# A written-out instruction order searched again, with GpSimd's memory-matrix product counted as making VectorE wait

## The chip, the cores and the metric

The kernel runs on one core of one Trainium2 chip. The core has five engines with queues of their own, each of which runs its instructions in order: TensorE (PE) multiplies matrices, VectorE (DVE), ScalarE (ACT) and GpSimd (POOL) do elementwise work, and SyncE (SP) issues the transfers (DMAs). The metric is the device time of one execution in microseconds, here 441.84 us as the median of three runs.

## What is computed

One transformer block over 2048 tokens of width 576. The attention half has 32 heads of width 18 and takes the tokens in four segments of 512. Every segment does causal softmax attention within itself, and reads a memory matrix that the earlier segments have filled:

```
for s in range(4):
    p = softmax(q_s k_s^T * scale + causal mask)
    a_dot = p v_s
    a_mem = phi(q_s) M / (phi(q_s) z + 1e-6)      # phi(t) = t + 1 if t > 0, else exp(t)
    out_s = g * a_mem + (1 - g) * a_dot           # g = sigmoid(beta), one number for each head
    M += phi(k_s)^T v_s ;  z += sum(phi(k_s))
h  = x + concat(out) wo
h2 = h + gelu(layernorm(h) w1 + b1) w2 + b2       # w1: 576 to 4608, w2: 4608 to 576
```

Data are bf16, sums and normalizations are in float32.

## The kernel before

**Stages.** The kernel is cut into 1904 operations. Each has a tag (stage and segment) and a name; the third number of a name counts its occurrences within the tag, from 0. Stage X normalizes and transposes x; P projects it to k, q and v; A is attention (`A00` to `A03` for the four token tiles of segment 0, `A1` to `A3` for the later segments); M sums the memory; B is the output projection, the residual and the second normalization; C is the first half of the MLP (`F1` its matmuls, `copy` the evictions, `gelu`); D is the second half (`F2`). The segments overlap: while segment 0 is in its MLP, segments 1 to 3 are in their projections and attention.

**Who sets the order.** No planner runs at the time of the launch that could choose. `TIMETABLE` gives every operation its engine and its place in one list of 1904 places: in `"A00mask": "g114 g147 g145 d104 ..."` the fourth mask (`A00mask.3`) is on VectorE (d) at place 104. The letters are p TensorE, a ScalarE, d VectorE, g GpSimd, s SyncE; w means that the operation is done in one instruction with its neighbour, u that ScalarE evicts with the gelu at once and no gelu follows. `schedule()` walks the list, gives out buffers (PSUM banks, tiles) in its order and emits the instructions; each engine's queue is the list cut down to its own operations. A place is therefore an order, not a time. The list was found beforehand by a search that used the same `schedule()` as its cost model.

**The model's rule on the shared port.** `Op` sets `rest`: how long an operation occupies the port to SBUF that VectorE and GpSimd share, that is its cost less a part at its start. `schedule()` lets an operation with a `rest` begin that part only when no operation with a `rest` on the other engine is in its own. An operation whose name stands in neither of the two lists has no `rest`, and neither waits nor makes wait.

**The memory-matrix product.** `mblk` (line 1085, stage M, three times) multiplies the summed memory by the gates into `MZ_blk`, four products of 18 partitions by 152 elements on GpSimd. `mem` (lines 1282 and 1285) is the matmul that reads it in the next segment's attention.

**Names that the steps below use.** `P..P` and `P..R` with k, q, v or o: the two halves of a projection of one token tile (lines 924, 954, 971). If both halves are neighbours in TensorE's order, they become one fused group, mostly eight full-row matmuls (line 954) and two of 64 rows (line 924); otherwise both are done in halves of the rows, 18 matmuls of 64 rows (line 924), and a small `pass` sits between them. `P..copy` evicts a projection; `fk` (line 1042), `ek` and `rk` make phi(k). `st0`, `exp`, `mask`, `val` are the scores, exponentials, causal masks and value products (lines 1151, 1102 and 1100, 1163 on VectorE and 1166 on GpSimd, 1182); in the later segments `st`, `exp`, `mask`, `val` (1311, 1336). `valT`, `rec`, `comb`, `swap` and `oT` bring the attention's output into the layout that the projection `Po`/`Ro` takes. `hadd` (1393) adds the residual; `stats`, `rstd` and `apply` are the normalization. `memset`, `ones`, `eps`, `gmz` prepare constants; `gates` is the sigmoid of beta.

Of the kernel before, what the change touches and what calls it, by code (L numbers as in the profile page):

```python
# [27 lines left out]
    "A00exp": "a 74 78 103 111",  # L28
    "A00mask": "g114 g147 g145 d104 g166 g192 d131 g190",
    "A00st0": "p 73 102",  # L30
    "A01comb": "g 200 211 250 234",
    "A01exp": "a151 a152 a155 a167 a179 w193 a175 a176",
    "A01mask": "g163 d156 g158 g162 d188 d198 g207 d194",
    "A01oT": "d 206 231 255 254 251",
    "A01rec": "d 186 202 223 217",
    "A01st0": "p 136 154 178 171",
    "A01swap": "g247 d242",
    "A01val": "p 172 208",
    "A01valT": "d 185 187 215 209",
    "A02comb": "g350 d399",  # L40
    "A02exp": "a197 a216 a260 w268 a218 a219 a235 w237 a288 w289 a308 a309 a338 a339",
    "A02mask": "g277 g278 g274 g281 g279 g305 g341 d340",
    "A02rec": "d 333 386",
    "A02st0": "p 196 252 210 229 275 296 320",
    "A02val": "p 304 325 352 354",
    "A02valT": "d 326 355",
    "A03comb": "g 487 513",
    "A03exp": "a361 a362 a390 w392 a369 a371 a400 a401 a413 a414 a423 w437 a463 w470",
    "A03mask": "d404 g375 g370 g372 g412 g416 g464 g478",
    "A03oT": "d 351 406 508 521 538",  # L50
    "A03rec": "d 430 481",
    "A03st0": "p 360 374 366 398 405 422 435",
    "A03swap": "d514 g523",
    "A03val": "p 417 418 477 479",
    "A03valT": "d 426 480",
    "A1comb": "d667 g694 g717 g782 g807 g816 g860 d883",
    "A1comb2": "g689 g703 g721 d783 g838 d824 d880 d888",
    "A1eg": "a 493 393 522 688 651 719 742 813",
    "A1exp": "a491 w501 a506 w516 a499 a500 a589 a594 a529 a530 a603 a610 a628 w631 a641 w650 a663 a679 a686 w693 a711 w723 a745 a751 "
        "a727 w734 a766 w770 a784 w789 a754 a757 a820 a826 a829 a839 a842 a849 a793 w799",  # L60
    "A1flip": "s 391 389 486 439 510 615 704 738",
    "A1mask": "g502 g536 g586 g584 g545 g605 d611 g604 g646 g671 g658 d672 g708 g700 g722 g714 d748 g752 g756 g773 d743 g781 g795 d790 "
        "g845 g830 g837 g840 g852 d850 g821 g809",
    "A1mem": "p 585 475 681 735 713 798 843 855",
    "A1memT": "d 593 476 691 736 718 808 844 856",
    "A1memfin": "g622 g647 g720 g767 d763 d823 d866 g882",
    "A1oT": "d 780 797 905 892 897",
    "A1pq": "d 550 428 642 710 662 771 803 831",
    "A1rec": "d 607 636 697 747 762 822 857 881",
    "A1rec2": "d 666 624 701 741 787 815 854 870",  # L70
    "A1rg": "g 454 410 596 547 660 765 778 788",
    "A1st": "p 483 505 498 582 528 602 625 640 657 685 707 744 726 764 777 749 814 828 836 792",
    "A1swap": "d 893 895",
    "A1val": "p 587 621 687 739 774 796 851 861",
    "A1valT": "d 599 623 698 740 776 811 853 869",
    "A2comb": "d1037 d983 d1143 g1096 g1175 g1190 g1246 d1230",
    "A2comb2": "d1039 d1067 d1146 g1097 d1188 g1193 d1259 d1236",
    "A2eg": "a 928 872 1053 976 1003 1085 1137 1160",
    "A2exp": "a899 a901 a858 w859 a886 a887 a874 a875 a906 a907 a993 w996 a1013 w1019 a985 a986 a1033 w1048 a1001 w1006 a1086 w1098 "
        "a1056 w1057 a1109 w1110 a1064 w1065 a1120 a1124 a1129 a1130 a1135 w1140 a1184 a1185 a1156 w1158 a1164 w1165",  # L80
    "A2flip": "s 825 847 891 961 1002 1040 989 1121",
    "A2mask": "d938 d915 d963 g903 d911 g958 g909 d923 g1042 d1032 g1041 g1007 g987 g1049 g1023 g1046 g1106 d1062 g1071 d1112 d1144 "
        "g1088 g1149 g1147 g1161 g1199 d1180 g1218 d1186 g1200 g1197 d1179",
    "A2mem": "p 998 946 1066 1044 1131 1145 1194 1202",
    "A2memT": "d 1011 960 1081 1047 1132 1148 1195 1212",
    "A2memfin": "g1038 d973 g1111 d1095 d1187 g1173 d1256 d1216",
    "A2oT": "d 1115 1178 1232 1263 1267",
    "A2pq": "d 951 910 1054 997 1075 1091 1170 1177",
    "A2rec": "d 1015 972 1090 1080 1154 1159 1231 1213",
    "A2rec2": "d 1036 982 1094 1073 1162 1152 1245 1229",  # L90
    "A2rg": "g 947 894 924 962 1074 1087 999 1176",
    "A2st": "p 898 848 885 873 904 988 1012 974 1020 1000 1084 1055 1105 1063 1116 1122 1134 1181 1155 1163",
    "A2swap": "g1238 d1265",
    "A2val": "p 970 959 1043 1050 1127 1150 1219 1201",
    "A2valT": "d 984 980 1072 1051 1128 1151 1226 1203",
    "A3comb": "g1426 d1376 d1481 d1503 d1556 g1528 g1642 d1611",
    "A3comb2": "g1427 d1445 g1499 d1504 g1572 d1563 g1643 g1617",
    "A3eg": "a 1211 1266 1337 1429 1474 1458 1543 1550",
    "A3exp": "a1220 w1224 a1250 w1254 a1262 a1269 a1334 a1336 a1279 a1280 a1389 a1390 a1372 a1384 a1396 a1397 a1412 a1415 a1362 a1366 "
        "a1443 w1444 a1423 w1424 a1463 w1467 a1492 a1495 a1452 w1454 a1507 a1510 a1518 a1524 a1532 w1539 a1567 a1569 a1547 a1548",  # L100
    "A3flip": "s 1141 1123 1282 1306 1208 1446 1387 1525",
    "A3mask": "g1268 d1341 d1356 d1313 d1351 g1350 d1342 g1298 d1418 g1410 g1393 g1406 d1409 g1416 g1398 g1403 d1491 d1468 d1461 d1493 "
        "g1479 d1496 g1482 g1455 d1590 g1554 g1553 g1540 g1565 g1570 d1579 d1587",
    "A3mem": "p 1340 1330 1425 1460 1526 1516 1586 1593",
    "A3memT": "d 1346 1331 1435 1473 1527 1523 1604 1600",
    "A3memfin": "g1365 g1364 g1477 d1502 g1571 g1542 g1619 d1602",
    "A3oT": "d 1451 1533 1646 1645 1644",
    "A3pq": "d 1253 1326 1405 1450 1498 1506 1578 1562",
    "A3rec": "d 1347 1354 1436 1489 1549 1541 1609 1601",
    "A3rec2": "d 1392 1375 1480 1478 1530 1515 1641 1610",  # L110
    "A3rg": "g 1227 1325 1377 1430 1209 1505 1559 1551",
    "A3st": "p 1217 1249 1261 1333 1278 1380 1371 1395 1408 1349 1437 1421 1459 1484 1447 1501 1517 1531 1566 1546",
    "A3swap": "d 1622 1621",
    "A3val": "p 1363 1352 1422 1431 1494 1497 1599 1595",
    "A3valT": "d 1374 1373 1441 1462 1500 1511 1640 1597",
    "B00Po": "p 256",
    "B00Ro": "p 258",
    "B00T": "p 306 348",
    "B00apply": "d 286",
    "B00copy": "a 315 349",  # L120
    "B00dma": "s 220 557",
    "B00hadd": "d264 w265",
    "B00pass": "d 257",
    "B00rstd": "g 285",
    "B00stats": "d 266",
    "B00tail": "d 287",
    "B01Po": "p 262",
    "B01Ro": "p 269",
    "B01T": "p 334 345",
    "B01apply": "d 322",  # L130
    "B01copy": "d 337 346",
    "B01dma": "s 248 436",
    "B01hadd": "d270 w271",
    "B01pass": "g 263",
    "B01rstd": "g 321",
    "B01stats": "d 298",
    "B01tail": "d 323",
    "B02Po": "p 554",
    "B02Ro": "p 560",
    "B02apply": "d 627",  # L140
    "B02dma": "s 497 896",
    "B02flip": "s 728 737",
    "B02hadd": "d568 w574",
    "B02pass": "g 559",
    "B02rstd": "g 626",
    "B02stats": "d 601",
    "B02tail": "d 680",
    "B03Po": "p 548",
    "B03Ro": "p 558",
    "B03apply": "d 620",  # L150
    "B03dma": "s 445 664",
    "B03flip": "s 684 702",
    "B03hadd": "d561 w562",
    "B03pass": "g 551",
    "B03rstd": "g 588",
    "B03stats": "d 567",
    "B03tail": "g 652",
    "B1Po": "p 912 925 929 940",
    "B1Ro": "p 914 931 935 942",
    "B1apply": "d 937 1025 1014 1083",  # L160
    "B1dma": "s 871 927 884 1028 953 1108 967 1010",
    "B1flip": "s 968 1021 1070 1092 1079 1076 1103 1104",
    "B1hadd": "d919 w920 d933 w943 d965 w966 d969 w971",
    "B1pass": "d913 g926 g930 d941",
    "B1rstd": "g 936 977 1004 1082",
    "B1stats": "d 921 952 991 1060",
    "B1tail": "g956 g1031 d1022 d1089",
    "B2Po": "p 1286 1290 1281 1303",
    "B2Ro": "p 1294 1300 1284 1305",
    "B2apply": "d 1309 1428 1464 1381",  # L170
# [169 lines left out]
    "omg": "g 174",  # L340
    "ones": "a 38 16",
    "tri": "g 5",
    "warm": "p 12 20 21",
    "wodma": "s 125 130",
    "x0b": "a 1",
    "x1": "s 2",
# [1391 lines left out]
```

## Time and profile before

| What | Value |
|---|---|
| runs of the kernel | 441.43, 441.84, 442.7 us (median 441.84) |
| the profiled execution, its own time | 441.8 us |
| its span, first to last instruction | 439.9 us |
| TensorE clock granted | 1.0 throughout |
| TensorE busy | 431.1 us, 98% of the span, 5069 matmuls |
| VectorE busy | 279.7 us, 64%, 578 instructions |
| ScalarE busy | 294.7 us, 67%, 314 instructions |
| GpSimd busy | 173.2 us, 39%, 331 instructions |
| transfers | 70.09 MB, mean 159 GB/s |

The profile's timeline has a row for each run of like instructions: start and duration in microseconds from the start of the span, engine, line of the kernel, operation, output from input with shapes, the count, and in brackets how long the engine stood idle before it and what ended that wait. Rows with a count over 1 cover all instructions of the run. The table by windows gives, for a stretch of the span, the busy time of PE, of its weight loads (PEld), of DVE, ACT and POOL, each with its number of instructions, then the granted clock, the share of the DMA engines and GB/s.

### The profile page before, as it was taken

What the parts mean: (1) busy time and instruction counts of PE and PEld (TensorE: products, weight loads), DVE (VectorE), ACT (ScalarE), POOL (GpSimd) and SP (SyncE); (2) the same over time, 40 slices, a digit from 0 to 9 for tenths busy, and PEclk for the clock granted to TensorE, in tenths of its full rate; (3) what the DMA queues carried; (4) which work ended last, traced back from release to release, by engine and by line L of the source; (5) the groups of instructions that cost most, each with busy time, mean ns of one, the idle gap of its engine ahead of it and who ended that gap; (6) DMA issues with size and microseconds to landing.
All of it is one profiled execution on the core that took longest, in us unless ns stands there. A gap on an engine that the chain in (4) does not pass through costs nothing.

```text
span 439.9 us, 12070 instructions
## 1 busy us (share of the span) xinstructions
PE 431.1 (98%) x5069; PEld 275.5 (63%) x5069; DVE 279.7 (64%) x578; ACT 294.7 (67%) x314; POOL 173.2 (39%) x331
## 2 busy tenths in 40 slices
PE   8988999999999999999999999999999999999997
PEld 5755678766677676654445766644457785446775
DVE  6999998897888885888797768876525021000111
ACT  6998888999977897677997877667842002656000
POOL 5686867655866252564331255352211110000000
PEclk9999999999999999999999999999999999999999
DMA  7899599899989965573746273616516553510102
GB/s 246 172 230 269 203 248 281 137 195 267 178 303 266 348 136 142 114 160 93 214 125 187 91 139 73 137 46 225 165 53 192 153 127 97 191 59 1 40 1 68
DMA packets 77126, 70.09 MB, mean 159 GB/s; under 512 B 58000, under 2 KB 64528, under 8 KB 77072
## 3 DMA queue, kind: packets, MB, share of 16 engines
q1 hardware_dynamic: 76928, 69.23, 60.8%
q8 instruction: 39, 0.64, 0.6%
q14 instruction: 15, 0.12, 0.1%
q10 hardware_dynamic: 144, 0.09, 0.1%
HBM read 42.30 MB, written 13.37 MB: 127 GB/s over the span
## 4 chain that ended last, share of the span: by engine, by line
PE 88%; DVE 7%; DMA 2%; issue 1%; ACT 1%; SPq 0%; DVEq 0%; ACTq 0%
PE bank L1563 31%; PE bank L1466 24%; PE bank L1509 7%; PE bank L924 7%; PE bank L954 5%; PE bank L1311 4%; PE bank L1336 3%; PE bank L971 1%; DMA w1g<-in_B_w_dram 1%; DVE ln L814 1%; PE bank L748 1%; DVE fk_pad L1042 1%; DMA ot<-in_B_b_dram 1%; PE bank L1285 1%; PE bank L1151 1%
## 5 line engine op out<-in xcount | busy, mean ns | idle before, releaser
L1563 PEld LDWEIGHTS <-hT 128*128 128x128 bf16 x1152 | 110.3, 98 | 34.1 <-issue 6.7
L1466 PE MATMUL bank<-xreg,w1g 64*128 64x512 bf16 x972 | 107.8, 376 | 0.0
L1102 ACT ACTIVATE pt<-bank 128x1024 bf16<-128x1024 f32 x88 | 85.2, 1022 | 24.2 <-PE bank L1311 14.9
L1466 PEld LDWEIGHTS <-w1g 64*128 64x128 bf16 x972 | 46.2, 94 | 56.7 <-issue 3.0
L1100 ACT ACTIVATE pt<-bank 128x2048 bf16<-128x2048 f32 x36 | 67.6, 1877 | 17.6 <-PE bank L1311 10.2
L1563 PE MATMUL bank<-w_lo,hT 128*128 128x288 bf16 x576 | 77.2, 286 | 0.0
L1563 PE MATMUL bank<-w,hT 128*128 128x288 bf16 x576 | 76.9, 286 | 0.1
L1576 DVE TENSOR_TENSOR ot<-bank,hc 128x288 bf16<-128x288 f32 x32 | 14.1, 449 | 82.0 <-PE bank L1563 73.4
L1325 POOL TENSOR_SCALAR_AFFINE_SELECT pt<-pt 128x512 bf16<-128x512 bf16 x63 | 43.5, 699 | 48.5 <-ACT pt L1102 27.1
L1472 ACT ACTIVATE hT<-bank,b_col 128x512 bf16<-128x512 f32 x36 | 22.3, 688 | 48.0 <-PE bank L1466 47.6
L1509 PE MATMUL bank<-xreg,w1g 64*128 64x256 bf16 x648 | 38.5, 269 | 0.8 <-DVE hT L1523 0.6
L1432 ACT ACTIVATE hT<-hT 128x4096 bf16<-128x4096 bf16 (+6 forms) x12 | 34.0, 2866 | 2.6 <-DVE hT L1488 2.5
L1509 PEld LDWEIGHTS <-w1g 64*128 64x128 bf16 x648 | 31.1, 94 | 7.0 <-issue 3.2
L1482 ACT ACTIVATE hT<-bank,b_col 128x512 bf16<-128x512 f32 x40 | 25.3, 693 | 10.6 <-PE bank L1466 10.2
L954 PE MATMUL bank<-hT,xreg 128*128 128x288 bf16 x228 | 31.4, 287 | 0.0
L924 PE MATMUL bank<-hT,xreg 64*128 64x288 bf16 x340 | 26.2, 284 | 0.5 <-DVE qk_pad L739 0.5
L954 PEld LDWEIGHTS <-xreg 128*128 128x128 bf16 x228 | 20.9, 98 | 7.5 <-issue 1.2
L1311 PE MATMUL bank<-qk 32*128 32x512 bf16 (+3 forms) x384 | 23.8, 301 | 0.1
L1291 DVE STREAM_TRANSPOSE t<-bank 128x512 f32<-128x512 f32 x24 | 16.9, 704 | 8.1 <-PE bank L1282 5.2
L924 PEld LDWEIGHTS <-xreg 64*128 64x128 bf16 x340 | 16.2, 94 | 9.2 <-issue 5.5
L1344 DVE STREAM_TRANSPOSE t<-bank 128x512 f32<-128x512 f32 x24 | 16.6, 696 | 6.4 <-PE bank L1336 6.3
L830 POOL TENSOR_TENSOR ln<-ln,mhalf 128x1 f32<-128x1 f32 x32 | 18.6, 580 | 2.7
(129 smaller groups left out, 574.0 us busy)
## 6 DMA issues: line engine op xcount, KB each, us to landing
w1g<-in_B_w_dram SPq DMA_DIRECT2D x41, 576.0 KB, 5.0
qkd<-qk_pad SPq DMA_DIRECT2D x12, 512.0 KB, 3.6
hd<-h SPq DMA_DIRECT2D x16, 288.0 KB, 3.0
hc<-hd SPq DMA_DIRECT2D x16, 288.0 KB, 3.4
w_lo<-in_B_w_dram SPq DMA_DIRECT2D x3, 864.0 KB, 7.2
w<-in_B_w_dram SPq DMA_DIRECT2D x3, 864.0 KB, 6.7
xb<-in_A_x_dram SPq DMA_DIRECT2D x16, 144.0 KB, 4.1
out_dram<-ot SPq DMA_DIRECT2D x15, 144.0 KB, 2.8
```

Source lines behind the costliest of these rows:

```text
L924: return nc.tensor.matmul(out=half(hf), lhsT=xTb.t[r, k, ts], rhs=wt[r, hf, k, :], start=start, stop=stop, skip_group_check=True)
L954: nc.tensor.matmul(out=half(hf), lhsT=xTb.t[:, k, ts], rhs=wt[:, hf, k, :], start=(k == 0 and b.form != "first"), stop=(k == n - 1 and b.f ...
L1100: nc.scalar.activation(out=pt.t[:], in_=banks_all[:, st[0].n:st[0].n + 4, :], func=ACT.Exp, scale=scale)
L1102: nc.scalar.activation(out=pt.t[:, 2 * j:2 * j + 2, :], in_=st[j].t[:], func=ACT.Exp, scale=scale)
L1311: nc.tensor.matmul(out=st[i // 2].t[:, i % 2, off:off + n_], lhsT=qk[rows, 1, kt * P:(kt + 1) * P], rhs=qk[rows, 0, kt * P:L], start=True, ...
L1325: nc.gpsimd.affine_select(out=blk, in_=blk, pattern=[[0, 4], [1, P]], compare_op=ALU.is_ge, fill=0.0, base=0, channel_multiplier=-1)
L1432: nc.scalar.activation(out=at, in_=at, func=ACT.Gelu_apprx_tanh)
L1466: nc.tensor.matmul(out=cc[w].t[:], lhsT=w1.t[rows, k, q, :], rhs=x2T[s].t[rows, k, :], start=(k == 0), stop=(k == ND - 1))
L1472: ready_f[f + w] = [add(pf - 12, {"act": 0.68}, lambda e, f=f, w=w, cc=cc: nc.scalar.activation(out=hT[:, :, f + w, :], in_=cc[w].t[:].rea ...
L1482: nc.scalar.activation(out=dst, in_=src, func=ACT.Identity if e == "act" else ACT.Gelu_apprx_tanh, bias=b)
L1509: nc.tensor.matmul(out=cc[w].t[:, q * 2 * P:(q + 1) * 2 * P], lhsT=w1.t[rows, k, q, :], rhs=x2T[s].t[rows, k, ts], start=(k == 0), stop=(k ...
L1563: nc.tensor.matmul(out=c.t[:, 0:c1 - c0], lhsT=hT[:, tl // 2, f, (tl % 2) * P:(tl % 2 + 1) * P], rhs=w2_c[ch][:, f - ch * WCH, c0:c1], sta ...
```

## The change

The operations, their instructions and their dependencies are the same. One name is added to the list of GpSimd operations that occupy the shared port, and the whole timetable is replaced by one that a search found under that rule, beginning from the former. Counted over the whole list, VectorE has six masks and five evictions more, GpSimd six masks fewer and four `comb2` more; ScalarE and the rest differ by a handful. Most of the change is order. All places are numbered anew, so nearly every row differs; the rows below are those that the text speaks of.

```diff
-        g = 0.15 if name in ("mask", "comb", "comb2", "memfin", "rg", "rk", "hc", "rstd", "eps", "memset", "swap") else 0.0
+        g = 0.15 if name in ("mblk", "mask", "comb", "comb2", "memfin", "rg", "rk", "hc", "rstd", "eps", "memset", "swap") else 0.0
...
-    "A00mask": "g114 g147 g145 d104 g166 g192 d131 g190",
+    "A00mask": "g 100 139 152 121 122 180 138 192",
-    "P01copy": "d123 d137 d93 a87 a98 a138",
+    "P01copy": "d120 d145 a99 a90 a106 a132",
-    "X00copy": "a25 d33 a31 a35",
+    "X00copy": "a30 d31 d36 a37",
-    "X00apart": "d19 a23 d28 a29",
+    "X00apart": "d12 a22 d26 a32",
-    "P00Pk": "p 37 41",
+    "P00Pk": "p 39 40",
-    "memset": "d8 g7 g36 d65 a26 a94 a58 a109 g427 g14 g328",
+    "memset": "d43 g9 g21 d2 a29 a35 a56 a34 g44 g14 g0",
-    "ones": "a 38 16",
+    "ones": "a 13 69",
-    "eps": "g 79 72 319 421 447 331 330 329",
+    "eps": "g 16 441 15 253 38 327 380 385",
-    "gates": "a95 d169",
+    "gates": "a124 d174",
-    "X1apply": "d 214 173",
+    "X1apply": "d 230 176",
-    "P1copy": "d232 a241 a344 d177 a189 a233 d313 a327 a297 a253 a293 d385",
+    "P1copy": "d234 a250 a344 d168 a204 a229 d314 a326 a304 a267 a295 d382",
-    "A02mask": "g277 g278 g274 g281 g279 g305 g341 d340",
+    "A02mask": "g259 g252 g316 g266 g291 g262 g338 d347",
-    "P1rk": "g 300 230 368 357",
+    "P1rk": "g 269 248 406 355",
-    "X2stats": "d 284 261 365 356",
+    "X2stats": "d 283 265 365 359",
-    "P1fk": "d 301 259 419 358",
+    "P1fk": "d 301 268 407 356",
-    "B00hadd": "d264 w265",
+    "B00hadd": "d270 w271",
-    "A02st0": "p 196 252 210 229 275 296 320",
+    "A02st0": "p 203 249 216 235 281 300 324",
-    "A02comb": "g350 d399",
+    "A02comb": "g 363 451",
-    "M0mblk": "g 448",
+    "M0mblk": "g 442",
-    "M1mblk": "g 484",
+    "M1mblk": "g 702",
-    "M2mblk": "g 1252",
+    "M2mblk": "g 965",
-    "X3apply": "d 457 532 539 443",
+    "X3apply": "d 454 530 561 504",
-    "P1Pq": "p 238 180 314 276",
+    "P1Pq": "p 238 188 320 284",
-    "P1Rq": "p 240 182 318 283",
+    "P1Rq": "p 242 195 322 286",
-    "P1Pk": "p 226 160 310 243",
+    "P1Pk": "p 231 162 306 241",
-    "P1Rk": "p 228 168 312 246",
+    "P1Rk": "p 233 165 313 247",
-    "A3val": "p 1363 1352 1422 1431 1494 1497 1599 1595",
+    "A3val": "p 1354 1360 1442 1445 1505 1507 1597 1598",
-    "C2F1": "p 1575 1573 1624 1616 1552 1544 1564 1536 1585 1582 1612 1606 1668 1630 1658 1628 1665 1635",
+    "C2F1": "p 1568 1588 1536 1548 1543 1550 1564 1571 1582 1600 1632 1658 1618 1610 1646 1626 1655 1669",
-    "A3oT": "d 1451 1533 1646 1645 1644",
+    "A3oT": "d 1589 1602 1622 1636 1638",
-    "A3swap": "d 1622 1621",
+    "A3swap": "a1625 d1631",
-    "B3Po": "p 1647 1666 1650 1648",
+    "B3Po": "p 1639 1657 1641 1670",
-    "B1Po": "p 912 925 929 940",
+    "B1Po": "p 908 911 927 943",
-    "B1Ro": "p 914 931 935 942",
+    "B1Ro": "p 912 922 934 945",
-    "B2Po": "p 1286 1290 1281 1303",
+    "B2Po": "p 1284 1295 1278 1292",
-    "B2Ro": "p 1294 1300 1284 1305",
+    "B2Ro": "p 1297 1300 1281 1301",
-    "B3Ro": "p 1652 1671 1656 1680",
+    "B3Ro": "p 1643 1665 1651 1672",
```

566 rows, old and new, of the table TIMETABLE are left out of this document.

## The prediction

> **What bounds the kernel now.** I read the page's engine shares first, then the busy times by windows, then TensorE's waits and the timelines around the longest.
>
> ```profile
> span 439.9 us, 12070 instructions
> ...
> PE 431.1 (98%) x5069; PEld 275.5 (63%) x5069; DVE 279.7 (64%) x578; ACT 294.7 (67%) x314; POOL 173.2 (39%) x331
> ```
>
> TensorE is the bound overall: 439.9 of span less 431.1 busy leaves 8.8 us. The windows say where they lie.
>
> ```profile
> 11.00:22.00 11.00, 10.92 (x164) 8.10 (x160) 10.08 (x23) 10.99 (x19) 6.94 (x22) 1.00 0.81 172
> 22.00:33.00 11.00, 9.30 (x213) 6.55 (x213) 10.76 (x24) 10.17 (x12) 9.12 (x18) 1.00 1.11 230
> 33.00:44.00 11.00, 9.60 (x130) 6.28 (x130) 10.70 (x24) 9.25 (x10) 7.18 (x15) 1.00 0.94 269
> 66.00:77.00 11.00, 10.41 (x214) 8.89 (x208) 9.87 (x20) 9.83 (x9) 7.77 (x20) 1.00 1.09 280
> 77.00:429.00 352.00, 351.63 (x3893) 218.96 (x3890) 208.31 (x419) 227.99 (x231) 119.54 (x202) 1.00 0.56 145
> ```
>
> TensorE idles 1.70 us between 22 and 33, 1.40 between 33 and 44, 0.59 between 66 and 77, and 0.37 in all of the 352 us that follow. Where it idles, VectorE is full (10.76 and 10.70 of 11) and ScalarE nearly so. A new order can therefore win in the first 77 us, by relieving VectorE; afterwards it can only lose, apart from what it takes from TensorE's own work. The end (last value of `F2`, its addition, its store) is in the same order in both lists, and is counted at nothing.
>
> **The rule itself.** The planner now lets `mblk` hold the port for its whole length. The trace shows what that hold does:
>
> ```profile
> 68.43 2.43 POOL L1085 TENSOR_TENSOR MZ_blk<-MZacc,gmz 18x152 bf16<-18x152 f32 x4
> 69.23 0.75 DVE L1275 SCALAR_TENSOR_TENSOR e<-e,r 128x512 bf16<-128x512 bf16 x1
> L1275 DVE SCALAR_TENSOR_TENSOR e<-e,r x24: 628/686/1165, 69.2 to 298.5; 128x512 bf16<-128x512 bf16 x24
> ```
>
> A two-input VectorE operation in the middle of `mblk` took 0.75 us against a median of 0.686: 0.06 lost, where the planner would charge up to 2. No TensorE wait follows it. So the rule corrects nothing that costs time; its effect is that the search found another list. I cost that list by its parts, from places and rows.
>
> **TensorE's own work.** Counted in the lists, 34 projections have both halves adjacent before and 31 after: `P1Pk.3`, `P1Pq.0`, `B1Po.0` and `B2Po.3` are split, `B3Po.3` is joined.
>
> ```profile
> 85.29 0.30 PE L924 MATMUL bank<-hT,xreg 64*128 64x288 bf16 x2
> 85.52 2.13 PE L954 MATMUL bank<-hT,xreg 128*128 128x288 bf16 x16
> 87.81 0.40 PE L1311 MATMUL bank<-qk 32*128 32x384 bf16 x8
> 88.14 2.38 PE L924 MATMUL bank<-hT,xreg 64*128 64x288 bf16 x36
> 90.36 0.78 PE L924 MATMUL bank<-wt_o,oT 64*128 64x288 bf16 x10
> ```
>
> Two fused projections run from 85.29 to 87.81, 1.26 us each; two split ones from 88.14 to 90.36, 1.11 each. Three times 0.15 is 0.45. A split one needs a `pass` in time, or another matmul between its halves; I take **-0.4** (0 to -0.6).
>
> **The stretch from 16 to 33 us.**
>
> ```profile
> 16.87 0.76 DVE L739 CAST v_aug<-bank 128x576 bf16<-128x576 f32 x1 [0.31 <-PE bank L924]
> 17.55 0.42 DVE L1163 TENSOR_TENSOR pt<-pt,tri 128x512 bf16<-128x512 bf16 x1
> 22.24 0.85 DVE L1163 TENSOR_TENSOR pt<-pt,tri 128x512 bf16<-128x512 bf16 x1
> 23.81 0.79 PE L924 MATMUL bank<-hT,xreg 64*128 64x288 bf16 x10 [0.49 <-DVE qk_pad L739]
> 26.86 0.47 DVE L1620 TENSOR_SCALAR g_bc<-g_bc 128x32 f32<-128x32 f32 x1
> 28.27 0.74 DVE L739 CAST qk_pad<-bank 128x576 bf16<-128x576 f32 x1
> 29.07 0.41 PE L1151 MATMUL bank<-qk 32*128 32x128 bf16 x16 [0.89 <-DVE qk_pad L739]
> 27.39 1.94 ACT L1102 ACTIVATE pt<-bank 128x1024 bf16<-128x1024 f32 x2 [0.46 <-PE bank L1151]
> 5.54 0.39 ACT L713 ACTIVATE fk_pad<-fk_pad 128x224 uint32<-128x224 uint32 x1
> 6.97 0.76 ACT L1608 ACTIVATE v_aug<-ident 128x128 bf16<-128x128 bf16 x1
> ```
>
> The first three rows are `P01copy.2`, `A00mask.3` and `A00mask.6`. The copy goes to ScalarE, the masks to GpSimd: 0.76 + 0.42 + 0.85 = 2.03 us leave VectorE ahead of its eviction that TensorE waits for at 23.81. The second wait, 0.89 at 29.07, is for `P1copy.3` at 28.27, which stands behind `gates` and `X1apply.1`, 26.86 to 28.27 or 1.41 us; in the new list it stands ahead of both. So both waits, 1.38 us, can go. What is late next is ScalarE. It gains that copy (some 0.7 by the row on VectorE) and `ones.1` (0.76, row at 6.97), which leaves a slot where ScalarE waited, and loses two clears of 0.39 (row at 5.54) to the start: 0.7 more in a stretch where it was busy 10.99 of 11 and whose only slack just before the second wait is 0.46, at 27.39. GpSimd has room for the two masks. I take **-0.7**, half of the 1.38 (0 to -1.38).
>
> **The start.** Here the moved work lands: on ScalarE two clears now stand ahead of `X00copy.3`, on GpSimd a large `memset` of `MZ_blk` stands first of all, and three `eps` with the second clear of `qk_pad` follow before the first `rstd`.
>
> ```profile
> 6.25 0.82 ACT L735 COPY xreg<-bank 128x384 bf16<-128x384 bf16 x2
> 6.50 2.74 PE L971 MATMUL bank<-hT,xreg 128*128 128x288 bf16 x21
> 50.13 0.95 POOL L715 MEMSET MZ_blk<- 128x1024 bf16 x1
> 50.40 0.99 DVE L848 TENSOR_SCALAR xn<-h,ln 128x576 bf16<-128x576 f32 x1
> L848 DVE TENSOR_SCALAR xn<-h,ln x16: 535/576/1070, 46.6 to 354.0; 128x576 bf16<-128x576 f32 x16
> ```
>
> The last of the two copies at 6.25 ends at 7.07; `P00Pk.1` needs it after the five matmuls of `P00Pk.0` (2.74 over 21 is 0.13 each, so at 7.15). Now ScalarE begins it two clears later, less one copy that went to VectorE: 0.78 - 0.41, so TensorE waits 0.3 to 0.4, and being busy from there to 22 us it passes the delay on. The two lower rows bound the memsets: beside one, a normalization took 0.99 instead of 0.576. Two of VectorE's `X00apart` steps lie beside such memsets now, at most 0.41 each. I take **+0.4** (0 to +1.2).
>
> **The stretch from 33 to 44 us.**
>
> ```profile
> 39.32 2.41 POOL L1166 TENSOR_SCALAR_AFFINE_SELECT pt<-pt 128x512 bf16<-128x512 bf16 x4
> 39.91 2.43 DVE L1042 SCALAR_TENSOR_TENSOR fk_pad<-ek,rk 128x576 bf16<-128x576 bf16 x1
> L1042 DVE SCALAR_TENSOR_TENSOR fk_pad<-ek,rk x12: 714/752/2428, 13.3 to 112.2; 128x576 bf16<-128x576 bf16 x12
> 44.02 0.40 PE L1151 MATMUL bank<-w_lo,qk 32*128 32x256 bf16 x8 [1.18 <-DVE h L1393]
> ```
>
> `P1fk.1` took 2.43 us against a median of 0.752: shut out, it seems, while GpSimd did four masks with no gap. `B00hadd` behind it on VectorE was late by those 1.68 us, and TensorE waited 1.18 for its bank. In the new list `X2stats.1` goes ahead of `P1fk.1`, and on GpSimd an `eps` breaks the run of masks; but another `P1rk` joins it, and `P1fk.1` still precedes `B00hadd`. I take **-0.5** (+0.3 to -1.18).
>
> **The stretch from 44 to 77 us.** `A02comb.1` goes to GpSimd, `X3apply.3` goes later on VectorE, `M1mblk` leaves GpSimd's busy stretch (place 484 to 702; its reader is in segment 2, far behind). Of the 0.59 idle I take **-0.2** (-0.59 to +0.3).
>
> **After 77 us.** TensorE had 0.37 idle, so a new list risks more than it can win. The tightest place that I find is the last projection. Before, seven steps of `C2F1` cover the way from the last values of `A3` to `B3Po`:
>
> ```profile
> 305.68 1.26 PE L1336 MATMUL bank<-pt,v_aug 128*19 128x512 bf16 x32
> 306.87 13.77 PE L1466 MATMUL bank<-xreg,w1g 64*128 64x512 bf16 x126
> 315.01 1.30 DVE L1365 STREAM_TRANSPOSE oT<-o_nat 128x512 bf16<-128x512 bf16 x2 [1.06 <-POOL o_nat L1355]
> 78.99 1.28 ACT L1100 ACT_TABLE_LOAD   x1
> ```
>
> The way took 306.94 to 316.31, 9.4 us, under 13.77. After, five steps cover it, 5/7 of 13.77 or 9.8 us: a margin of 0.4. ScalarE also changes its function table 15 times instead of 13 (counted in the lists), 1.28 each, not on TensorE's path if its banks come free. I take **+0.4** (-0.3 to +2.5).
>
> **The sum.** -0.4 - 0.7 + 0.4 - 0.5 - 0.2 + 0.4 = -1.0, from the profiled execution's 441.8 us (0.04 under the median of the runs): **440.8 us**. All good ends together give -4.1, all bad ones +4.3; they are independent, so neither is likely.
>
> **The rivals.** First, *the relief pays in full*: the waits of 1.38 and 1.18 go and ScalarE keeps up. The -0.7 becomes -1.38, the -0.5 becomes -1.18, the start's +0.4 hides in waits that TensorE had anyway (0): -1.0 - 0.68 - 0.68 - 0.4 = -2.8, **439.0 us**. For it speaks that VectorE is the full engine in both windows; against it ScalarE's 10.99 and 10.17.
>
> Second, *ScalarE takes the place of VectorE*: neither of the two stretches gains, only TensorE's own work and the 0.2 remain against the start and the late margin: -0.4 + 0.4 - 0.2 + 0.4 = +0.2, **442.0 us**. The waits would read ScalarE's exponentials (lines 1100, 1102) in place of the evictions.
>
> Third, and slower than before, *GpSimd's masks shut VectorE out more often*. Two masks more on GpSimd lengthen its runs, and the price of one run is on record: 1.68 us in front of a two-input operation. If two more such lock-outs fall between 16 and 44 us, they cost 3.4 and undo the two gains' 1.2 in part: 440.8 + 3.4 = **444.2**; with one, 442.5. From two on it is slower beyond what can be measured. For it speaks that GpSimd is busy 9.12 of 11 already from 22 to 33; against it that most of that stretch's VectorE operations read a bank and one tile. The Trainium skill's page "SBUF — State Buffer" (Who interferes with whom) calls the shared pair an exclusive lock that is held for a whole instruction, so that the loser blocks until it ends. By that rule `P1fk.1` would have waited for one mask, a quarter of 2.41 or 0.6 us, and two more lock-outs would end at 442.0, within; the trace's 1.68 goes beyond it, and `mblk` would have stopped the operation at 69.23, which it did not, by the 0.75.
>
> **How the numbers follow.** I give the forecast 0.45, full relief 0.20, ScalarE as next bound 0.15, lock-outs or a late stall of that size 0.20. For the three signs, 0.3% or 1.3 us is about what a measurement of this kernel can tell from no change: faster means under 440.5 and slower over 443.2. The forecast's own range is 439.8 to 442.0, and two fifths of it lie under 440.5: 0.18 of faster, with full relief 0.38. Slower gets the last case, whose mild form with one lock-out stays within, and a little from elsewhere: 0.20. The rest, 0.42, is no change. The range of 8 in 10 runs from full relief to between one and two lock-outs: 439.0 to 443.6.
>
> **What would show it.** Right: 580 matmuls on line 924 and 252 on line 954 (31 fused projections, of which 29 have eight full-row matmuls and two of 64 rows, two have ten full-row ones, and 29 split ones of 18); the waits at 23.8 and 29.1 gone or halved; the wait for `hadd` near 44 under 0.7; TensorE's idle time from 22 to 44 near 2 us instead of 3.1; a wait of some 0.3 us near 7 us on line 971. Wrong: a `fk` of over 2 us in other places, exponentials as the releaser of TensorE's waits between 24 and 44, or idle time of over 1 us anywhere behind 77 us, near the last projection first of all.

## The result, and the profile after

The changed kernel takes 440.69 us (median of 22 runs, 439.62 to 441.91); the kernel before, in 22 runs beside it, 441.88. The ratio is 0.9975, 95% interval 0.9966 to 0.9983: 1.1 us less (0.8 to 1.5). That is a real gain, but by the 0.3% set above it counts as no change. The forecast was 440.8.

The profiled execution took 441.13 us, with a span of 439.4. First the page of the kernel after (span, busy time of each engine), then its table by windows with the columns of before:

```profile
span 439.4 us, 12125 instructions
...
PE 431.0 (98%) x5092; PEld 276.9 (63%) x5093; DVE 276.5 (63%) x585; ACT 298.5 (68%) x318; POOL 175.3 (40%) x332
```

```profile
11.00:22.00 11.00, 10.96 (x165) 8.37 (x163) 8.23 (x19) 10.36 (x15) 6.03 (x16) 1.00 0.76 156
22.00:33.00 11.00, 10.11 (x221) 7.34 (x219) 10.63 (x23) 10.91 (x14) 9.92 (x19) 1.00 1.09 271
33.00:44.00 11.00, 10.12 (x166) 6.51 (x158) 9.97 (x27) 9.41 (x11) 7.30 (x19) 1.00 0.71 207
66.00:77.00 11.00, 10.81 (x238) 8.43 (x232) 10.52 (x21) 10.61 (x9) 8.16 (x19) 1.00 1.03 282
77.00:429.00 352.00, 350.71 (x3864) 219.89 (x3862) 207.79 (x427) 230.23 (x235) 119.61 (x199) 1.00 0.57 145
```

VectorE did lose work to ScalarE and GpSimd, and TensorE's idle time from 22 to 44 us fell from 3.10 to 1.77. But behind 77 us it rose from 0.37 to 1.29. TensorE's waits (engine, line, releaser; total, times, longest) say why:

```profile
PE bank L954 <- DMA xreg<-xn: 1.1, 1, 1.1
PE bank L748 <- PEq L1722: 0.8, 1, 0.8
PE bank L971 <- DMA hT<-in_A_w_dram: 0.7, 1, 0.7
PE bank L1151 <- DVE MZacc L1076: 0.5, 1, 0.5
PE bank L924 <- ACT pt L1102: 0.5, 1, 0.5
PE bank L865 <- ACT xn L846: 0.3, 1, 0.3
```

The waits for `h` (1.18 us) and for `qk_pad` (0.89 and 0.49) are gone. In their place stand two transfers and an exponential, and the wait for `MZacc`, an eviction on VectorE, grew from 0.2 to 0.5. (The 0.8 on line 748 stands in both kernels.)

Idle time in a window isn't yet a gain, since the windows of the two kernels hold different work. So I compared when the same TensorE step begins in both traces (the same group of one line's matmuls, counted from the first). After minus before, in us:

| start before | step | after minus before | change since the row above |
|---|---|---|---|
| 13.02 | first scores, L1151 | +0.94 | +0.94 |
| 33.74 | scores, L1151 | +0.34 | -0.60 |
| 37.05 | scores, L1151 | +0.97 | +0.63 |
| 47.08 | scores behind B00hadd, L1151 | -0.68 | -1.65 |
| 77.33 | values, L1182 | -1.35 | -0.67 |
| 87.81 | scores of segment 1, L1311 | 0.00 | +1.35 |
| 330 to the end | L1466, L1563 | -0.56 | -0.56 |

The new list loses a microsecond at the start, wins 0.6 up to 33.7 us and has lost that again by 37, wins 2.3 between 37 and 77 us, loses more than one again at 87 us, and wins half a microsecond in the long rest. This pair shows less than the medians (0.56 against 1.1); the transfers' waits, which differ between executions (below), may be the reason.

### The profile page after: what moved, and what is told of

Same layout as the page of the kernel before. It is cut to its first block, busy times and chain, and to the rows that moved or that the text cites. A ratio compares the mean times of both kernels' runs of the same rounds, so it can differ in the third digit from the quotient of the medians.

```text
span 439.4 us, 12125 instructions
## 1 busy us (share of the span) xinstructions
PE 431.0 (98%) x5092; PEld 276.9 (63%) x5093; DVE 276.5 (63%) x585; ACT 298.5 (68%) x318; POOL 175.3 (40%) x332
## 4 chain that ended last, share of the span: by engine, by line
PE 86%; DVE 5%; DMA 4%; issue 2%; ACT 2%; SPq 1%; DVEq 0%; ACTq 0%
PE bank L1563 32%; PE bank L1466 24%; PE bank L924 7%; PE bank L1509 6%; PE bank L954 6%; PE bank L1311 4%; PE bank L1336 3%; DMA xreg<-xn 2%; DMA hT<-in_A_w_dram 1%; ACT pt L1102 1%; PE bank L1151 1%; DMA qk<-qk_pad 1%; PE bank L1285 1%; PE bank L1282 1%; DVE hT L1523 1%
## 5 line engine op out<-in xcount | busy, mean ns | idle before, releaser
L1563 PEld LDWEIGHTS <-hT 128*128 128x128 bf16 x1152 | 110.5, 98 | 33.8 <-issue 5.9
L1466 PE MATMUL bank<-xreg,w1g 64*128 64x512 bf16 x972 | 108.4, 376 | 0.0
L1102 ACT ACTIVATE pt<-bank 128x1024 bf16<-128x1024 f32 x92 | 89.3, 1023 | 23.7 <-PE bank L1311 18.9
L1466 PEld LDWEIGHTS <-w1g 64*128 64x128 bf16 x972 | 47.1, 94 | 55.7 <-issue 3.0
L1563 PE MATMUL bank<-w_lo,hT 128*128 128x288 bf16 x576 | 77.4, 286 | 0.2 <-issue 0.2
L1563 PE MATMUL bank<-w,hT 128*128 128x288 bf16 x576 | 76.8, 286 | 0.0
L1100 ACT ACTIVATE pt<-bank 128x2048 bf16<-128x2048 f32 x34 | 63.8, 1876 | 14.5 <-PE bank L1311 8.5
L1325 POOL TENSOR_SCALAR_AFFINE_SELECT pt<-pt 128x512 bf16<-128x512 bf16 x55 | 38.3, 709 | 37.1 <-ACT pt L1102 25.1
L1549 POOL TENSOR_TENSOR hc<-hc,b_bc 128x576 f32<-128x576 f32 x8 | 10.7, 1340 | 78.0 <-DMA hc<-hd 78.0
L1432 ACT ACTIVATE hT<-hT 128x512 bf16<-128x512 bf16 (+7 forms) x16 | 36.0, 2304 | 0.1
L954 PE MATMUL bank<-hT,xreg 128*128 128x288 bf16 x212 | 29.4, 287 | 1.2 <-DMA xreg<-xn 1.1
L924 PE MATMUL bank<-hT,xreg 64*128 64x288 bf16 x372 | 28.1, 284 | 0.5 <-ACT pt L1102 0.5
L1549 DVE TENSOR_TENSOR hc<-hc,b_bc 128x576 f32<-128x576 f32 x8 | 6.4, 796 | 31.2 <-DMA hc<-hd 31.2
L954 PEld LDWEIGHTS <-xreg 128*128 128x128 bf16 x212 | 19.4, 98 | 8.3 <-DMA xreg<-xn 1.4
L1311 PE MATMUL bank<-qk 32*128 32x512 bf16 (+3 forms) x384 | 23.8, 301 | 0.0
L1323 DVE TENSOR_TENSOR pt<-pt,tri 128x512 bf16<-128x512 bf16 x41 | 19.4, 489 | 5.5 <-ACT pt L1102 2.9
```

Source lines behind the costliest of these rows:

```text
L924: return nc.tensor.matmul(out=half(hf), lhsT=xTb.t[r, k, ts], rhs=wt[r, hf, k, :], start=start, stop=stop, skip_group_check=True)
L954: nc.tensor.matmul(out=half(hf), lhsT=xTb.t[:, k, ts], rhs=wt[:, hf, k, :], start=(k == 0 and b.form != "first"), stop=(k == n - 1 and b.f ...
L1100: nc.scalar.activation(out=pt.t[:], in_=banks_all[:, st[0].n:st[0].n + 4, :], func=ACT.Exp, scale=scale)
L1102: nc.scalar.activation(out=pt.t[:, 2 * j:2 * j + 2, :], in_=st[j].t[:], func=ACT.Exp, scale=scale)
L1311: nc.tensor.matmul(out=st[i // 2].t[:, i % 2, off:off + n_], lhsT=qk[rows, 1, kt * P:(kt + 1) * P], rhs=qk[rows, 0, kt * P:L], start=True, ...
L1325: nc.gpsimd.affine_select(out=blk, in_=blk, pattern=[[0, 4], [1, P]], compare_op=ALU.is_ge, fill=0.0, base=0, channel_multiplier=-1)
```

## The experiments

With the former timetable the changed rule gives every engine the same instructions in the same order. From the 3159th of the 5069 matmuls on (235.6 us in the trace of before), though, 1755 write to other PSUM banks, since `schedule()` chooses a free bank by its modelled times; no run prices that. Up to that time all effect is the list's, and every experiment edits lists. The diffs show the places as each list has them; places behind an insertion shift by one.

**Which part of the list?** The new list up to `A1mem.1` (place 473, near 76 us) and the former order from there, and the reverse.

```diff
 early_new, against the new list
-    "X2flip": "s 370 436 438 505",
+    "X2flip": "s370 s436 s438 s475",
-    "B3Po": "p 1639 1657 1641 1670",
+    "B3Po": "p1647 p1666 p1650 p1648",
 late_new, against the new list
-    "X00dma": "s 47 45 51 42",
+    "X00dma": "s13 s15 s32 s10",
-    "P1fk": "d 301 268 407 356",
+    "P1fk": "d301 d259 d419 d358",
```

> The new list up to the memory product A1mem.1 (77 us), then the operations that are left in the former order. The transposition X2flip.3, which TensorE waits for at 85 us in the new list, comes early here, as in the former. Theory (the gain is made by VectorE's relief between 22 and 77 us, where the new trace leads by 1.35 us): 1.2 to 1.5 us faster than before, some 440.5. Rival (the early part nets nothing, since both traces are level again at 88 us, and the gain is TensorE's own work in what follows): no difference from before, 441.7 to 442.0.

Measured: 440.74 us, ratio 0.9977 (0.9966 to 0.9988). The first part alone gives as much as the whole list. It doesn't follow that the second part is worth nothing: this run is spared the new list's wait for `X2flip.3`. In its profile it waits 1.3 us for the q weights where the new list waited 0.7, and it loses 0.68 where the halves meet (its like steps lead by 1.11 us at 77 and by 0.43 at 87.8). Against flip_early below, which has that transposition early too and the new order to the end, it is 0.7 us slower by the ratios, with intervals that overlap a little.

> The former list up to A1mem.1, then the operations that are left in the new order. Theory: only TensorE's own work and order behind 88 us are won, the 0.56 us by which the new trace leads from 216 us on: 0.4 to 0.7 us faster than before, some 441.3. Rival (the gain is late): all of the 1.2 us, some 440.7.

Measured: 445.57 us, ratio 1.0085 (1.006 to 1.0111), slower than expected. The second of these lines of its timeline carries it:

```profile
88.38 2.38 PE L924 MATMUL bank<-hT,xreg 64*128 64x288 bf16 x36
93.75 3.25 PE L924 MATMUL bank<-wt_o,oT 64*128 64x288 bf16 x28 [3.00 <-ACT pt L1102]
```

The two halves don't fit where they meet: a projection waits 3.00 us for a bank that an exponential still holds. That exponential stands on ScalarE behind a step (line 1271) for which ScalarE idled 4.64 us, until a transfer landed (`qk<-qkd`): a late transfer again. And the wait costs more than its length: the granted clock of TensorE, 1.00 from 77 to 92 us, is 0.79 from 92 to 94, 0.50 from 94 to 96, 0.86 from 96 to 98, and 1.00 again from there. Behind the wait that is 2.8 us at half clock, or 1.4 us lost by estimate. Like steps stand at +0.23 at 87.81 and +4.77 at 97.73, and at +3.98 from 289 us on. The run therefore gives no price for the late part as a whole. In its trace the new order is worth some 0.8 behind 98 us.

**What do the two transfers cost?** In the new list `X00dma.0`, the first half of the q weights, is loaded behind `X00dma.1`, the second; and `X2flip.3`, a transposition that `P2Pv.3` (place 523) needs, went from place 425 to 505. The timeline of the kernel after at both places:

```profile
8.77 0.53 PE L971 MATMUL bank<-hT,xreg 128*128 128x288 bf16 x3
10.02 2.00 PE L971 MATMUL bank<-hT,xreg 128*128 128x288 bf16 x15 [0.72 <-DMA hT<-in_A_w_dram]
84.27 1.16 PE L954 MATMUL bank<-hT,xreg 128*128 128x288 bf16 x8
86.50 1.15 PE L954 MATMUL bank<-hT,xreg 128*128 128x288 bf16 x8 [1.07 <-DMA xreg<-xn]
```

```diff
 q_first
-    "X00dma": "s 47 45 51 42",
+    "X00dma": "s45 s47 s51 s42",
 flip_early
-    "X2flip": "s 370 436 438 505",
+    "X2flip": "s370 s436 s438 s439",
```

> The new list with one exchange: the first half of the q weights is loaded ahead of the second, as formerly. TensorE's wait of 0.72 us for that load at 10 us should go. Theory (TensorE is busy from there to 24 us, so what is lost at the start is passed on): 0.6 to 0.8 us faster than the new list, some 440.0. Rival (ScalarE and VectorE set the pace between 24 and 36 us, and the start's delay is hidden by waits there): under 0.2 us faster, some 440.6.

Measured: 439.95 us, ratio 0.9963 (0.9951 to 0.9975), as the theory had it. Like steps begin 0.60 earlier than in the new list at 14 us, and keep it.

> The new list with one move: the transposition X2flip.3 goes from place 505 to just behind X2flip.2 (438), near its former place. TensorE's wait of 1.07 us at 85 us should go. Theory (nothing hides it, TensorE is full on both sides): 0.8 to 1.1 us faster than the new list, some 439.7. Rival (the profiled execution was 0.4 us over the median of the new kernel's runs, so in an ordinary run that transposition is late by less): 0.3 us or less, some 440.4.

Measured: 439.74 us, ratio 0.9960 (0.9948 to 0.9972), the gain of the theory. Like steps gain 1.25 between 77 and 88 us.

> The new list with both moves: the q weights' first half first, X2flip.3 early. Theory (both waits are on TensorE's path, and what one gives the other does not take): the sum of the two, 1.4 to 1.8 us faster than the new list, some 439.0. Rival (the time gained at the start is waited for again between 24 and 44 us): as the early transposition alone.

Measured, with both edits: **438.81 us** (438.61 to 439.28), ratio 0.9933 (0.992 to 0.9945). This beats both kernels: 3.0 us under the kernel before, 1.9 under the change. Its waits and its last window:

```profile
PE bank L748 <- PEq L1722: 0.8, 1, 0.8
PE bank L1151 <- DVE MZacc L1076: 0.5, 1, 0.5
PE bank L924 <- ACT pt L1102: 0.5, 1, 0.5
```

```profile
77.00:429.00 352.00, 351.97 (x3870) 220.97 (x3866) 206.83 (x425) 229.19 (x235) 120.22 (x199) 1.00 0.57 144
```

No transfer is left among TensorE's waits, and of 352 us behind 77 it idles 0.03. Neither wait is constant. The wait for the q weights stands in all four profiles with the new list's loads (0.7 after, 1.3 early_new, 0.6 flip_early, 0.9 no_relief), and in three of the ten with the halves in order (0.9 in eps_behind, 0.3 in late_new, 0.2 in relief_alone). The wait for `X2flip.3` stands in one of three profiles that have it at place 505: after, but not q_first or no_relief.

**Is relieving VectorE worth anything?** `A00mask.3`, `A00mask.6` and `P01copy.2` back on VectorE in the new list; the same three taken off it in the former list; and back on it with both transfers mended.

```diff
 no_relief, against the new list (fixed_no_relief has both_fixed's edits too)
-    "A00mask": "g 100 139 152 121 122 180 138 192",
+    "A00mask": "g100 g139 g152 d121 g122 g180 d138 g192",
-    "P01copy": "d120 d145 a99 a90 a106 a132",
+    "P01copy": "d120 d145 d99 a90 a106 a132",
 relief_alone, against the former list
-    "A00mask": "g114 g147 g145 d104 g166 g192 d131 g190",
+    "A00mask": "g114 g147 g145 g104 g166 g192 g131 g190",
-    "P01copy": "d123 d137 d93 a87 a98 a138",
+    "P01copy": "d123 d137 a93 a87 a98 a138",
```

> The new list with A00mask.3, A00mask.6 and P01copy.2 back on VectorE, at their new places. Theory (these 2.03 us off VectorE are what opens the stretch from 22 to 44 us): 0.6 to 1.4 us slower than the new list, some 441.7. Rival (the order of P1copy.3 ahead of the gates and of P1fk.1 behind the statistics makes the gain, and ScalarE, freed of the copy, is glad of it): within 0.3 us of the new list or faster.

Measured: 440.36 us, ratio 0.9967 (0.9956 to 0.9978). No slower than the new list.

> The former list with A00mask.3 and A00mask.6 on GpSimd and P01copy.2 on ScalarE, at their former places. Theory: the wait of 0.49 us at 23.8 us goes, the one of 0.89 us at 29.1 us shrinks; 0.3 to 0.8 us faster than before. Rival (ScalarE, busy 10.99 of 11 us from 11 to 22, becomes the bound): no difference or slower.

Measured: 441.28 us, ratio 0.9992 (0.9982 to 1.0001). No gain that can be told from none. Its waits and the two places in its timeline:

```profile
PE bank L1151 <- DVE h L1393: 1.2, 1, 1.2
...
PE bank L1151 <- DVE qk_pad L739: 0.6, 1, 0.6
PE bank L924 <- POOL mark_pool L930: 0.6, 1, 0.6
PE bank L1182 <- DVE pt L1163: 0.5, 1, 0.5
```

```profile
25.88 0.79 PE L924 MATMUL bank<-hT,xreg 64*128 64x288 bf16 x10 [0.57 <-POOL mark_pool L930]
...
29.48 0.41 PE L1151 MATMUL bank<-qk 32*128 32x128 bf16 x16 [0.62 <-DVE qk_pad L739]
```

The wait at 23.8 is gone, but the next projection waits 0.57 for `mark_pool`, the small `pass` on GpSimd, which has two masks more in this list.

> The new list with both moves, and in addition A00mask.3, A00mask.6 and P01copy.2 back on VectorE. If handing these three over is worth nothing or less, as the run of the new list without them says, the time is 438.4 to 438.9. If that run was only the lucky absence of the wait for X2flip.3, which is mended here on both sides, the three cost VectorE their 2.03 us in part: 439.2 to 439.9.

Measured: 439.53 us, ratio 0.9943 (0.9931 to 0.9955), 0.7 over both_fixed (0.4 by the ratios), with intervals that overlap. Like steps in the two profiles differ by +0.26 at 33 us, by -0.04 at 37, and by +0.24 from 110 us to the end. The three operations are worth 0.2 us by the traces, at most some 0.7 by the medians, of the 2.03 us of VectorE's time; what they win up to 33 us is gone by 37.

**What does the shut-out `fk` cost?** Three edits of the former list, each of which leaves all else alone: `P1fk.1` behind `B00hadd`; `X2stats.1` ahead of `P1fk.1`; and an `eps`, three tiny memsets of GpSimd, between the first and the second of the four masks.

```diff
 fk_behind
-    "P1fk": "d 301 259 419 358",
+    "P1fk": "d301 d265 d419 d358",
 stats_ahead
-    "X2stats": "d 284 261 365 356",
+    "X2stats": "d284 d259 d365 d356",
 eps_between
-    "eps": "g 79 72 319 421 447 331 330 329",
+    "eps": "g79 g72 g320 g275 g447 g332 g331 g330",
```

> The former list with P1fk.1 moved behind B00hadd, past the run of four masks on GpSimd that held it up for 1.68 us. Theory: TensorE's wait of 1.18 us at 44 us goes, and fk takes about 0.75 us: 0.7 to 1.1 us faster than before, as far as VectorE, full until 66 us, lets TensorE keep it. Rival (the lead is waited for again between 44 and 77 us, where VectorE is at 21.2 of 22 us): under 0.3 us.

Measured: 440.55 us, ratio 0.9972 (0.9961 to 0.9984): as much as the whole new list. Like steps stand at +0.08 at 39.9 us, -0.86 at 47.1 and -1.42 from 77.3 on. The wait for `h` fell from 1.18 to 0.3.

> The former list with X2stats.1 (0.8 us on VectorE) ahead of P1fk.1 and nothing else, which is the order of the new list at this place without its eps. Theory: P1fk.1 begins 0.9 later, still within the run of masks, ends when the run ends, and only X2stats.1 is out of the way behind it: the wait of 1.18 at 44.0 falls to some 0.3, time down by 0.4 to 0.9, 440.9 to 441.4. Rival, that the place of X2stats.1 does nothing because the eviction waits for the masks all the same: within 0.3 of the kernel before.

Measured: 440.71 us, ratio 0.9972 (0.9963 to 0.9981), a little more than expected. GpSimd and VectorE in its timeline:

```profile
39.69 2.41 POOL L1166 TENSOR_SCALAR_AFFINE_SELECT pt<-pt 128x512 bf16<-128x512 bf16 x4
42.08 0.71 POOL L829 TENSOR_SCALAR ln<-ln 128x1 f32<-128x1 f32 x1
```

```profile
41.22 1.49 DVE L1042 SCALAR_TENSOR_TENSOR fk_pad<-ek,rk 128x576 bf16<-128x576 bf16 x1
42.63 0.74 DVE L1393 TENSOR_TENSOR h<-bank,xb 128x576 f32<-128x576 f32 x1
```

`fk` begins inside the third mask, is passed by the fourth, and gets in at its end; the small `rstd` behind the masks is now the one that is held up, 0.71 us where the other one that follows takes 0.22. `B00hadd` begins at 42.63 instead of 43.23.

> The former list with one eps (three tiny memsets of GpSimd) moved from place 421 to a place behind the first of the four masks that ran without a gap at 39.3 us. Theory, that an unbroken run of masks keeps the shared port from VectorE and any other short operation between them lets it in: P1fk.1 takes under 1.2 us instead of 2.43, the wait of 1.18 for B00hadd at 44.0 falls under 0.3, and the time falls by 0.7 to 1.2, as with P1fk.1 moved behind B00hadd: 440.4 to 441.0. Rival, that the length of the masks counts and not their being unbroken: P1fk.1 still takes over 1.7 us, and the time stays within 0.3 of the kernel before's.

Measured: 440.26 us, ratio 0.9962 (0.995 to 0.9974), the largest gain that one move of the former list gave, and by the medians more than the whole new list's. GpSimd, VectorE and the window:

```profile
39.62 0.64 POOL L1166 TENSOR_SCALAR_AFFINE_SELECT pt<-pt 128x512 bf16<-128x512 bf16 x1
40.32 0.50 POOL L1596 MEMSET MZ_blk<- 21x8 bf16 x3
40.90 1.82 POOL L1166 TENSOR_SCALAR_AFFINE_SELECT pt<-pt 128x512 bf16<-128x512 bf16 x3
```

```profile
40.22 0.72 DVE L1042 SCALAR_TENSOR_TENSOR fk_pad<-ek,rk 128x576 bf16<-128x576 bf16 x1
...
42.03 0.76 DVE L1393 TENSOR_TENSOR h<-bank,xb 128x576 f32<-128x576 f32 x1
```

```profile
33.00:44.00 11.00, 10.69 (x153) 6.78 (x149) 10.53 (x28) 10.03 (x11) 8.31 (x19) 1.00 0.95 269
```

`fk` takes 0.72 us beside the memsets, as it does in the seven profiles of the new list that have an `eps` there (0.70 or 0.71). The wait for `h` is gone, and TensorE idles 0.31 us of this window instead of 1.40. Like steps stand at -1.15 at 47 us and -1.44 at the end.

Then the mirror: in the version with both transfers mended, the `eps` that stands between the masks was moved behind them.

```diff
 eps_behind, against both_fixed
-    "eps": "g16 g442 g15 g253 g38 g327 g380 g385",
+    "eps": "g16 g442 g15 g266 g38 g327 g380 g385",
```

> The new list with both moves (first half of the q weights first, X2flip.3 early), and the eps that stood between the masks of A02 moved behind the fourth of them. The mirror of the last run. Theory of the unbroken run: P1fk.1 again takes over 1.7 us, B00hadd behind it is late, and the time rises by 0.5 to 1.2 over the 438.81 of both moves: 439.3 to 440.0. Rival: P1fk.1 keeps its 0.7 and the time stays at 438.8, within 0.3.

Measured: 439.46 us, ratio 0.9944 (0.993 to 0.9958). The median lies 0.5 to 0.65 us over both_fixed, with intervals that overlap. In the profiled execution, the slowest of the six (440.65), the cause of the theory is not to be seen:

```profile
41.30 3.00 POOL L1166 TENSOR_SCALAR_AFFINE_SELECT pt<-pt 128x512 bf16<-128x512 bf16 x4
```

```profile
41.91 0.71 DVE L1042 SCALAR_TENSOR_TENSOR fk_pad<-ek,rk 128x576 bf16<-128x576 bf16 x1
42.61 0.76 DVE L1393 TENSOR_TENSOR h<-bank,xb 128x576 f32<-128x576 f32 x1
```

This time `fk` got in at the end of the first mask and the masks waited: 3.00 us for four instead of 2.41. Like steps stand at +1.15 against both_fixed already at 13 us, where this profile waits 0.9 for the q weights, and at +1.22 at 53 us: the masks cost nothing here. What raised the median stays open. So "an unbroken run keeps `fk` out" is too strong. With the `eps` between the masks it got in at once in all eight profiles; without, it may lose (three profiles of the former list's order, three mask ends passed), lose once and then win (stats_ahead), or win at once.

## Why the prediction was right

The time was right, 440.8 against 440.69, and no change by the bound of 0.3% was the likeliest of the three signs. That the median lies 0.1 us from the forecast is luck in part: the terms missed by up to a microsecond, in both directions, and the one pair of traces gives -0.56 for the sum of -1.0. Two of the signs that I had named for being wrong came as well: exponentials among the releasers between 24 and 44 us, and over 1 us of idle time behind 77. The trace's column is from the table of like steps.

| term | predicted | the traces show |
|---|---|---|
| the start | +0.4 | +0.94 |
| 16 to 33 us | -0.7 | -0.60 by 33.7 us, +0.03 by 37 |
| 33 to 44 us | -0.5 | -1.45, from 37 us on |
| 44 to 77 us | -0.2 | -0.67 |
| TensorE's own work | -0.4 | -0.20 near 38 us, the rest not told apart |
| after 77 us | +0.4 | +0.79, with the own work there |

**The rule itself.** I read its price from VectorE's side alone, as 0.06 us, and that reading was wrong. Two rows of the kernel before show the other payer:

```profile
L1085 POOL TENSOR_TENSOR MZ_blk<-MZacc,gmz x12: 468/480/831, 68.4 to 229.6; 18x152 bf16<-18x152 f32 x12
228.19 0.97 DVE L1275 SCALAR_TENSOR_TENSOR e<-e,r 128x512 bf16<-128x512 bf16 x1
```

The product of `mblk` that began at 69.49, beside the VectorE operation that I had looked at, took 0.83 us against a median of 0.48: GpSimd was held up by 0.35. At 228.19 the like VectorE operation took 0.97 against 0.686, and the next product 0.83 again. So the two engines do hold each other up at `mblk`, by some 0.3 us and on either side, and what I held against an exclusive lock there, in the third rival, does not stand. That this costs TensorE nothing does: no wait of TensorE names `MZ_blk` before or after.

**TensorE's own work** was right in kind. Lines 924 and 954 have 372 + 208 = 580 and 212 + 40 = 252 matmuls, as counted in the lists:

```profile
L954 PE MATMUL bank<-hT,xreg 128*128 128x288 bf16 x212 | 29.4, 287 | 1.2 <-DMA xreg<-xn 1.1
L924 PE MATMUL bank<-hT,xreg 64*128 64x288 bf16 x372 | 28.1, 284 | 0.5 <-ACT pt L1102 0.5
L924 PE MATMUL bank<-wt_o,oT 64*128 64x288 bf16 x208 | 14.9, 283 | 0.0
L954 PE MATMUL bank<-wt_o,oT 128*128 128x288 bf16 x40 | 5.6, 287 | 0.0
```

The size can be read at one place. `P1Pq.0` and `P1Pk.3` stand next to each other, fused before and split after; the first two of these rows are of before, the last two of after:

```profile
37.38 0.30 PE L924 MATMUL bank<-hT,xreg 64*128 64x288 bf16 x2
39.92 0.40 PE L1151 MATMUL bank<-w_lo,qk 32*128 32x256 bf16 x8
38.35 2.42 PE L924 MATMUL bank<-hT,xreg 64*128 64x288 bf16 x36
40.70 0.40 PE L1151 MATMUL bank<-w_lo,qk 32*128 32x256 bf16 x8
```

The two took 2.54 us before and 2.35 after: 0.1 for each, not 0.15. Behind 88 us the lists differ by one split projection alone (`B1Po.0` and `B2Po.3` against `B3Po.3`). So of the -0.56 there some 0.15 is idle time (0.37 before; 1.29 less the 1.07 of the transposition after), some 0.1 the split, and the cause of the rest stays open.

**The start** was right in sign and wrong in reason. TensorE waited 0.26 us for ScalarE at `X00`'s transposes (line 865, releaser `xn`), but stats_ahead, with the former list, has the same wait with 0.30, and both_fixed, with the new list's places of ScalarE, reaches the first scores 0.09 us ahead of the kernel before. ScalarE's two clears thus cost nothing that the traces show. What they do show is 0.72 us for the q weights' first half, loaded second. I had weighed ScalarE's and GpSimd's queues there and not SP's, though the change holds the row of `X00dma`: the step that failed is the list of what moved.

**16 to 33 us** came nearly in size, and then did not last. Both waits for VectorE's evictions went, as forecast, and up to 33.7 us the like steps gained 0.60. But waits for exponentials came in their place, 0.16 at 25.14 and 0.52 at 29.85, the mark that I had given for the second rival. Right behind the stretch a wait for `MZacc` grew (third row below; 0.17 at the same step before), and the next projection waited 0.13 for another exponential within its row:

```profile
25.14 0.41 PE L1151 MATMUL bank<-qk 32*128 32x128 bf16 x16 [0.16 <-ACT pt L1102]
...
29.85 0.30 PE L924 MATMUL bank<-hT,xreg 64*128 64x288 bf16 x2 [0.52 <-ACT pt L1102]
...
34.89 0.38 PE L1151 MATMUL bank<-w_lo 32*128 32x128 bf16 x13 [0.54 <-DVE MZacc L1076]
```

By 37 us nothing is left of the 0.60. The step that failed is that a wait of TensorE which goes is time won: for what lasts of this stretch, the second rival was right, though VectorE (`MZacc`) and ScalarE (10.91 of 11) share the place of the next bound. relief_alone shows the like, with GpSimd's `pass` among the successors. The first reason, VectorE's 2.03 us, was tested and is worth 0.26 us here at most (fixed_no_relief); the second, the place of `P1copy.3`, was not tested alone. Taking half of the 1.38 between two ends was a guess.

**33 to 44 and 44 to 77 us** had the right mechanism and were too small. I took -0.5 of at most 1.18, as `P1fk.1` still precedes `B00hadd`. The three edits of the former list are worth 0.94, 0.96 and 1.45 between 39.9 and 47.1 us and 1.50, 1.51 and 1.76 by 77.3. The whole new list is worth 1.45 between the same two steps, as much as the best of these single moves; which of its own moves there does it is not shown, since taking the `eps` out again (eps_behind) cost nothing at this place. So the gain does not end with the wait for `h`; what follows from `B00hadd` (normalization, the first steps of the MLP) carries some 0.3 to 0.6 more into the stretch where I had seen only 0.59 of idle time. My -0.2 priced that stretch by its own moves and not by what arrives earlier from the one ahead.

**After 77 us** the sign was right and the place wrong. The last projection shows no wait, and the two table loads more (16 in the table of groups instead of 14) cost TensorE nothing visible. The loss is `X2flip.3` at 86.5 us, 1.07, a transfer that none of my steps held. SP's queue is the one that I left out at both places.

**The rivals.** The lock-outs did not multiply: the longest `fk` after took 1.09 us, against 2.43 before, and no other operation on VectorE between 11 and 110 us exceeds its median by more than 0.4 us.

```profile
L1042 DVE SCALAR_TENSOR_TENSOR fk_pad<-ek,rk x12: 705/750/1087, 14.1 to 112.2; 128x576 bf16<-128x576 bf16 x12
```

Full relief, at 439.0, came near what the list gives once its two transfers are mended (438.81), but by another way than that rival had it.

## What to carry to other kernels

When an order is searched anew, go through every queue for what moved, the transfers' queue first: two transfers put too late for their readers cost 1.9 us here, of the 3.0 us that the other moves together gained, and no busy time shows them. A single operation at twice or three times its median, with the bound engine's longest wait close behind, is worth an edit of its own: one move of a tiny memset in the former list gave at least as much as a new search over 1904 operations. And measure a gain by when the same later step begins, not by the idle time of a window.

## What the runs showed that was not expected

**Who wins the shared port is not decided by the gapless run alone.** In the following table are the recorded starts of `fk` and of the mask that it met at the first mask's end, in us:

| run | fk | mask | who went first |
|---|---|---|---|
| before | 39.914 | 39.921 | mask, and two more |
| late_new | 40.245 | 40.251 | mask, and two more |
| relief_alone | 40.731 | 40.742 | mask, and two more |
| eps_behind | 41.915 | 41.898 | fk, mask held 0.59 |

They lie within 0.02 us, and the one recorded first lost each time. What decides it stays open. The Trainium skill's page "SBUF — State Buffer" (Who interferes with whom) says that the order of issue decides who blocks, and for a whole instruction. This case's traces don't settle that: a hold of 1.68 us over three masks goes beyond one instruction, and the recorded starts give the opposite order, but no run shows whether a recorded start is the moment of issue. The same section of the Trainium skill says that a two-input VectorE instruction contends only with a GpSimd instruction that reads SBUF, not with one that only writes. The 0.72 beside the memsets of eps_between agrees with that.

**A transfer's wait comes and goes with the execution.** The same transposition at the same place held TensorE for 1.07 us in one profile and not at all in two others; the medians (0.9 for its move alone, 0.7 by the ratios) suggest that it often does.
